# Token tiles 2 and 3 turned on TensorE instead of by DMA, and a new order of loads and queries, in the opening of an attention and MLP kernel

## The chip, the cores and the metric

The kernel runs on one core of one Trainium2 chip. The metric is the device time of the execution in microseconds. Before the change its median is 1055.08 us of 3 runs (1054.37 to 1055.83).

## What is computed

The reference, cut to what matters (S = 2048 tokens, D = 1024, 32 heads of 32, F = 3584, all bf16):

```python
def reference(A_x, A_wqkv, A_wo, B_x, B_w1, B_b1, B_w2, B_b2):
    x = A_x
    xn = _layernorm(x)
    # A: attention on xn
    q, k, v = split_heads(xn @ A_wqkv)
    p = softmax(q @ k.T * 32 ** -0.5)           # 32 heads, 2048 x 2048 each
    s = merge_heads(p @ v) @ A_wo
    # B: MLP on layernorm(xn)
    h = gelu(_layernorm(xn) @ B_w1 + B_b1)
    g = silu(h @ B_w2 + B_b2)
    return x + s * g
```

## The kernel before

The kernel lists its operations with what each reads and writes, lets a small scheduler written in Python put them in an order per engine while it is built, and then emits that order with semaphore waits. The order is static: nothing is chosen on the chip. The durations that the scheduler assumes (for a DMA, for an engine's operation) only serve to choose the order.

In the opening, x is loaded in 16 tiles of 128 tokens. For each tile DVE (VectorE) takes mean and variance, GpSimd the power -0.5, and DVE writes the normalized tile in bf16 (tile 2's sums are taken on ACT, ScalarE). The matmuls need the tile turned (features on the partitions), and for that there are two ways:

```python
def tr_item(t, half=None):              # on TensorE, in a PSUM bank
    ...
        for dc in range(lo, lo + n):
            ins = e.transpose(bankb(b)[:, dc * 128:(dc + 1) * 128],
                              xnb[t % 4][:, dc * 128:(dc + 1) * 128], ident[:])
    ...
    if half == 1 or t in EVD:           # and a copy to the turned tokens xnT
        dve(lambda e: e.tensor_copy(dst, src()), ...)
    else:
        act(lambda e: e.activation(dst, src(), ACT.Copy), ...)
# ...
for t in (lo, lo + 1):                  # the tiles of pair n
    if t < TD:                          # TD = 2 before
        pro_q.append(tr_item(t))
    else:                               # by DMA
        add("SP", lambda e, t=t: e.dma_start_transpose(
                out=xnT[:, :, t * 128:(t + 1) * 128], in_=xnb[t % 4]),
            1290, 0, [("xnb", t % 4)], [("xnT", t, h) for h in range(2)], 0,
            sem=f"tp{t % 4}", nbytes=262144)
pro_q.append(k_pair_item(n, False))     # keys of the pair, first head group
if n == 1:
    pro_q.append(q_pair_item(1))        # queries of the second 256 tokens
if n >= VLAG:                           # VLAG = 2
    pro_q.append(v_item(0, n - VLAG, "pro"))   # values, two pairs behind
```

Heads are worked four at a time (a head group), queries in groups of 256 tokens, keys in pairs of tiles (256 keys). A unit is one query group against one key pair: its scores are 8 matmuls on PE (TensorE, L1167), and its exponentials two activations of 128x1024 on ACT (L1181). The first two query groups go through the key pairs together, so that each new pair gives ACT two units, or four activations; query group 2 starts when pair 7, the last, is through. The kernel has 8 head groups x 8 query groups x 8 pairs = 512 units, so 1024 activations. Products with the values are 8 matmuls (L723), while matmuls of the projections, MLP and output (L728) are put between the scores.

```python
for tq in range(1, 4):                  # queries of the first head group, 512 tokens each
    it = qk_item(0, 0, tq, wq0, 16 * tq - 12)
    if tq == 1 and QE:                  # QE = 0 before
        ...
    plan.queues["proj"].append(it)

def load_w1(p):                         # first weights of the MLP, in two halves of 256 KB
    ...
        dma(f"w1{gi}{i}", ..., [xnop[XW + 2 * p]] if p < 3 else [])   # waits for a normalized tile
def load_w2(q, r):                      # second weights, 448 KB each
    ...
    dma(f"w2{i}", lambda e: e.dma_start(w2r[:, i], src), 580000, [], [("w2", i)])
```

Where PE would find nothing to do early in the kernel, the order may have a matmul of the identity as filler. All DMA is issued from SP (SyncE).

Of the kernel before, what the change touches and what calls it, by code (L numbers as in the profile page):

```python
# [42 lines left out]
NCUT = 2  # L43
HALF = 1
NU = 22
QE = 0
AS = (2,)
FILL = 300
ADJ2 = 0
TD = 2  # L50
XA = 8
XB = 5
XW = 9
ENGS = ("PE", "ACT", "DVE", "POOL", "SP")


# [18 lines left out]
class _Plan:  # L75
# [54 lines left out]
    def run(self, total_units, dense_slack):  # L130
# [28 lines left out]
        def commit(o, t):  # L159
            e = o.eng  # L160
            o.start = t
            if e == "SP":
                if o.prio >= 5:
                    for x in reversed(order["PE"]):
                        if x.fin <= t:
                            o.deps[x] = True
                            break
                tf[e] = t + o.occ
                state["bw"] = max(state["bw"], t) + o.nbytes / 380.0
                o.fin = state["bw"] + {"w1": WLAT, "w2": WLAT, "tp": 2800.0, "x0": 2050.0, "x1": 2000.0, "x2": 2500.0}.get(o.sem[:2], 2300.0)  # L170
            else:
                tf[e] = t + o.occ
                o.fin = t + o.occ + o.lat
            order[e].append(o)
            self.seq.append(o)
            release(o, t)
            wake(tf[e], e)
# [379 lines left out]
def bass_recurrent_scan__mha_block__mixer_channel_mlp__prompt_kernel(  # L557
# [39 lines left out]
    with ExitStack() as st:  # L597
# [112 lines left out]
        def pool(fn, occ, R, W, prio=3):  # L710
            return add("POOL", fn, occ, PL, R, W, prio)

        def dma(sem, fn, nbytes, R, W, prio=3, extra=()):
            return add("SP", fn, 430, 0, R, W, prio, sem=sem, nbytes=nbytes, extra=extra)

        def chunk(item, fn, occ, R, mode="f", W=()):
            o = add("PE", lambda e, fn=fn, item=item: fn(e, item.bank), occ, TL, R, W, item=item, mode=mode)
# [36 lines left out]
        def load_v(pr):  # L754
            src = A_wqkv[:, 2 * D + pr * 256: 2 * D + (pr + 1) * 256].rearrange("(c p) n -> p c n", p=128)
            dma("wv", lambda e: e.dma_start(wv, src), 850000, [], [("wv",)])
# [2 lines left out]
            load_x(t)  # L759
        wk0 = load_qk(0, 1)  # L760
        wq0 = load_qk(0, 0)
        for t in range(XF, 6):
            load_x(t)
        load_v(0)
        for t in range(6, XA):
            load_x(t)
        pool(lambda e: e.iota(iota_i, pattern=[[1, 128]], base=0, channel_multiplier=-1), 300, [], [("iota",)])
        dve(lambda e: e.tensor_single_scalar(ident[:], iota_i, 0, op=ALU.is_equal), 220, [("iota",)], [("ident",)], 0)
        dve(lambda e: e.memset(ones[:], 1.0), 90, [], [("ones",)], 0)
# [35 lines left out]
        def q_pair_item(n):  # L805
            return pair_item(n, (0,))
# [77 lines left out]
        for n in range(NPR):  # L884
            for t in (2 * n, 2 * n + 1):
                if t in AS:

                    junk = yT[:, 4:8, :].rearrange("p c t -> p (c t)")
                    act(lambda e, t=t: e.activation(junk, xst[t], ACT.Copy, scale=-1.0 / 32768, accum_out=lnp[:, t, 2:3]),
                        c_acts(1024) + 93, [XS(t)], [("yT", 2), ("yT", 3), ("st", t, 0)], 1)  # L890
                    act(lambda e, t=t: e.activation(junk, xst[t], ACT.Square, bias=lnp[:, t, 2:3], scale=1.0 / 32,
                                                    accum_out=mv[:, t, 1:2]),
                        c_acts(1024) + 186, [XS(t), ("st", t, 0)], [("yT", 2), ("yT", 3), ("st", t, 1)], 1)
                    dve(lambda e, t=t: e.tensor_scalar_mul(mv[:, t, 0:1], lnp[:, t, 2:3], -32.0), 65,
                        [("st", t, 0), ("st", t, 1)], [("mv", t)], 1)
                else:
                    for c in range(2):
                        dve(lambda e, t=t, c=c: e.bn_stats(stats[:, t, c, :], xst[t][:, c * 512:(c + 1) * 512]),  # L898
                            600, [XS(t)], [("st", t, c)], 1)
                    dve(lambda e, t=t: e.bn_aggr(mv[:, t, :], stats[:, t, :, :].rearrange("p c s -> p (c s)")),  # L900
                        150, [("st", t, 0), ("st", t, 1)], [("mv", t)], 1)
                for k in range(XA, NT):
                    if max(0, k - XB) == t:
                        load_x(k, [("st", t, 0)])
            lo, hi = 2 * n, 2 * n + 2
            if n == 0:
                for t in (0, 1):
                    dve(lambda e, t=t: e.tensor_scalar_add(lnp[:, t:t + 1, 0], mv[:, t:t + 1, 1], EPS), 90, [("mv", t)], [("ve", 0, t)], 0)
                    pool(lambda e, t=t: e.tensor_tensor(lnp[:, t:t + 1, 1], lnp[:, t:t + 1, 0], mhalf[:, t:t + 1], op=ALU.pow),
                         650, [("ve", 0, t), ("mhalf",)], [("rs", 0, t), ("rs", 0)], 0)  # L910
                    dve(lambda e, t=t: e.tensor_scalar(xnb[t], xst[t], mv[:, t, 0:1], lnp[:, t, 1:2],
                                                       op0=ALU.subtract, op1=ALU.mult), 455,
                        [XS(t), ("mv", t), ("rs", 0, t)], [("xnb", t)], 0.5)
                pro_q += [tr_item(0), qk_tile_item(0), tr_item(1, 0), tr_item(1, 1), qk_tile_item(1)]
                if VLAG == 0:
                    pro_q.append(v_item(0, 0, "pro"))
                continue
            dve(lambda e, lo=lo, hi=hi: e.tensor_scalar_add(lnp[:, lo:hi, 0], mv[:, lo:hi, 1], EPS), 90,
                [("mv", lo), ("mv", lo + 1)], [("ve", n)], 1)
            dve(lambda e, lo=lo, hi=hi: e.tensor_scalar_mul(lnp[:, lo:hi, 4], mv[:, lo:hi, 0], -1.0), 65,  # L920
                [("mv", lo), ("mv", lo + 1)], [("nm", n)], 1)
            pool(lambda e, lo=lo, hi=hi: e.tensor_tensor(lnp[:, lo:hi, 1], lnp[:, lo:hi, 0], mhalf[:, lo:hi], op=ALU.pow),
                 700, [("ve", n), ("mhalf",)], [("rs", n)], 0)
            pool(lambda e, lo=lo, hi=hi: e.tensor_tensor(lnp[:, lo:hi, 5], lnp[:, lo:hi, 4], lnp[:, lo:hi, 1], op=ALU.mult),
                 200, [("nm", n), ("rs", n)], [("nb_", n)], 0)
            for t in (lo, lo + 1):
                if t in DN:
                    xnop[t] = dve(lambda e, t=t: e.tensor_scalar(xnb[t % 4], xst[t], mv[:, t, 0:1], lnp[:, t, 1:2],
                                                                 op0=ALU.subtract, op1=ALU.mult), 455,
                                  [XS(t), ("mv", t), ("rs", n)], [("xnb", t % 4)], 0.5)  # L930
                    continue
                xnop[t] = pool(lambda e, t=t: e.tensor_scalar(xnb[t % 4], xst[t], lnp[:, t, 1:2], lnp[:, t, 5:6],
                                                    op0=ALU.mult, op1=ALU.add), 950,
                     [XS(t), ("nb_", n), ("rs", n)], [("xnb", t % 4)], 1)
            for t in (lo, lo + 1):
                if t < TD:
                    pro_q.append(tr_item(t))
                else:

                    add("SP", lambda e, t=t: e.dma_start_transpose(out=xnT[:, :, t * 128:(t + 1) * 128], in_=xnb[t % 4]),  # L940
                        1290, 0, [("xnb", t % 4)], [("xnT", t, h) for h in range(2)], 0, sem=f"tp{t % 4}", nbytes=262144)
            pro_q.append(k_pair_item(n, False))
            if n == 1:
                pro_q.append(q_pair_item(1))
            if n >= VLAG:
                pro_q.append(v_item(0, n - VLAG, "pro"))
        for n in range(NPR - VLAG, NPR):
            pro_q.append(v_item(0, n, "pro"))
        q_at = len(pro_q)

        pool(lambda e: e.tensor_tensor(lnp[:, :, 2], mv[:, :, 1], lnp[:, :, 1], op=ALU.mult), 150,
             [("rs", n) for n in range(NPR)], [("s2",)], 2)
# [22 lines left out]
        def load_w1(p):  # L975
            gi = p % NW1R
            pi = p % NW1
            for i in range(2):
                src = B_w1[i * 512:(i + 1) * 512, pi * 256:(pi + 1) * 256].rearrange("(c p) f -> p c f", p=128)
                dma(f"w1{gi}{i}", lambda e, i=i, src=src: e.dma_start(w1r[gi][:, 4 * i:4 * i + 4], src), 332000, [], [("w1", gi, i)], 3,  # L980
                    [xnop[XW + 2 * p]] if p < 3 else [])

        def load_w2(q, r):
            i = nw2["n"] % NW2R
            nw2["n"] += 1
            src = B_w2[r * 7 * 128:(r + 1) * 7 * 128, q * 256:(q + 1) * 256].rearrange("(f p) n -> p f n", p=128)
            dma(f"w2{i}", lambda e: e.dma_start(w2r[:, i], src), 580000, [], [("w2", i)])
            return i

        def b1_item():  # L990
# [349 lines left out]

        for tq in range(1, 4):
            it = qk_item(0, 0, tq, wq0, 16 * tq - 12)
            if tq == 1 and QE:
                it.kind, it.due = "pro", 1
                pro_q.insert(q_at - QE, it)
                continue
            plan.queues["proj"].append(it)
            it.after = 1000
# [144 lines left out]
```

The softmax here doesn't subtract the row's maximum and nothing guards it: scores larger than these inputs give would overflow.

## Time and profile before

| | before |
|---|---|
| median of 3 runs | 1055.08 us |
| profiled span | 1055.5 us |
| busy: PE / ACT / DVE / GpSimd | 1028.4 / 1013.0 / 960.5 / 14.8 us |
| instructions | 32143 |
| DMA moved | 160.16 MB |

The profile is one execution. Its page gives the busy time of each engine, the span in 40 equal slices (a digit is the busy share of a slice in tenths, PEclk the clock that TensorE was granted), the chain of work that ended last, and groups of instructions by line: count, busy time, mean duration, and after the second bar the idle time before them with what ended it. Durations of pipelined instructions overlap: an activation of 128x1024 shows some 1.02 us alone, but a row of them comes every 0.92 us. A matmul of 256 columns shows 0.27 us, and a row of them comes about every 0.11 us. Names such as `big<-gw` say what is written from what: `big` holds the turned tokens, `gw` and `yT` the normalized tiles before turning, `qk` the weights, queries and keys of the first head group, `w1r` and `w2r` the MLP's weights, `P` the exponentials, `hT` and `w2r` early on also x.

### The profile page before, as it was taken

The page shows a single profiled execution, that of the slowest core. Times are in us where ns is not written, and L with a number is a line of the kernel's source. Part 1 is how long each engine was busy: PE and PEld are TensorE (multiplying, and loading weights), DVE is VectorE, ACT ScalarE, POOL GpSimd, SP SyncE. Part 2 cuts the span into 40 slices and gives each one's busy share as a digit, 9 for nine tenths or more (in the row PEclk, how much of TensorE's full clock was granted, in tenths as well). Part 3 has the DMA queues.
Part 4 walks back from the last instruction along what each step waited for, and adds up shares of the span by engine and source line. Part 5 has one row for each costly group of instructions (what it writes and reads, how often), then busy time and mean ns, then how long its engine had stood idle before and what let it go on. Part 6 is the DMA issues. An engine that isn't in the chain of part 4 may idle for free.

```text
span 1055.5 us, 32143 instructions
## 1 busy us (share of the span) xinstructions
PE 1028.4 (97%) x14326; PEld 637.6 (60%) x14326; DVE 960.5 (91%) x1454; ACT 1013.0 (96%) x1104; POOL 14.8 (1%) x28
## 2 busy tenths in 40 slices
PE   8899999999999999999999999999999999999997
PEld 4445566656676566656676566656665667664442
DVE  7659999999899999999999999999989999979897
ACT  4699999999999999999999999999999999999993
POOL 1200000000000000000000000000000000000000
PEclk9999999999999999999999999999999999999999
DMA  9945256743276356634465456434475587673431
GB/s 234 186 111 148 79 161 191 197 127 96 70 221 173 108 148 185 173 109 113 117 189 161 113 164 183 141 104 116 143 198 161 171 236 221 205 221 95 137 102 60
DMA packets 302371, 160.16 MB, mean 152 GB/s; under 512 B 40218, under 2 KB 293146, under 8 KB 302234
## 3 DMA queue, kind: packets, MB, share of 16 engines
q1 hardware_dynamic: 302234, 158.12, 53.8%
q8 instruction: 112, 1.84, 0.7%
q14 instruction: 25, 0.20, 0.1%
HBM read 142.35 MB, written 12.06 MB: 146 GB/s over the span
## 4 chain that ended last, share of the span: by engine, by line
ACT 85%; PE 11%; DMA 2%; DVE 1%; SPq 0%; issue 0%; DVEq 0%
ACT P L1181 79%; PE ps L728 7%; ACT ut L1042 5%; PE ps L723 2%; PE ps L1167 2%; ACT gw L1078 1%; DMA big<-gw 1%; DMA big<-yT 1%; DMA hT<-in_A_x_dram 0%; DVE w1r L1328 0%; DVE ut L898 0%; SPq L742 0%; PE ps L866 0%; DVE V L1331 0%; DVE V L1328 0%
## 5 line engine op out<-in xcount | busy, mean ns | idle before, releaser
L1181 ACT ACTIVATE P<-ps 128x1024 bf16<-128x1024 f32 x1024 | 964.8, 1241 | 20.3 <-PE ps L1167 20.2
L1211 DVE TENSOR_TENSOR PA<-P 128x2048 bf16<-128x2048 bf16 x245 | 297.7, 1217 | 17.8 <-ACT P L1181 16.5
L728 PE MATMUL ps<-yT,w1r 128*128 128x256 bf16 x1792 | 232.5, 273 | 0.6 <-DVE yT L1010 0.6
L728 PE MATMUL ps<-w2r,hT 128*128 128x256 bf16 x1792 | 225.0, 273 | 1.8 <-DVE xb L1027 0.6
L728 PEld LDWEIGHTS ps<-yT,w1r 128*128 128x128 bf16 x1792 | 162.7, 98 | 56.2 <-issue 30.6
L728 PEld LDWEIGHTS ps<-w2r,hT 128*128 128x128 bf16 x1792 | 163.8, 98 | 50.8 <-issue 29.6
L723 PE MATMUL ps<-P,V 128*32 128x256 bf16 x4096 | 144.7, 274 | 1.2 <-DVE xb L1027 0.7
L728 PE MATMUL ps<-big,qk 128*128 128x512 bf16 (+2 forms) x568 | 133.4, 361 | 6.1 <-DMA big<-gw 3.8
L1216 DVE TENSOR_TENSOR PA<-PA 128x1024 bf16<-128x1024 bf16 x201 | 135.6, 681 | 1.2
L728 PE MATMUL ps<-qk,big 128*128 128x256 bf16 (+1 forms) x736 | 128.0, 308 | 0.9 <-DMA qk<-in_A_wqkv_dram 0.8
L723 PEld LDWEIGHTS ps<-P,V 128*32 128x32 bf16 x4096 | 97.2, 96 | 34.2 <-issue 23.6
L1167 PE MATMUL ps<-qk 32*128 32x256 bf16 x2048 | 108.6, 274 | 6.0 <-ACT P L1181 5.4
L1167 PE MATMUL ps<-QKT 32*128 32x256 bf16 x2048 | 101.7, 273 | 1.4 <-ACT P L1181 1.2
L728 PEld LDWEIGHTS ps<-qk,big 128*128 128x128 bf16 x736 | 65.2, 98 | 44.8 <-issue 19.2
L1027 DVE TENSOR_TENSOR xb<-ps,b1T 128x512 bf16<-128x512 f32 x112 | 76.4, 684 | 8.4 <-PE ps L728 7.1
L728 PEld LDWEIGHTS ps<-big,qk 128*128 128x128 bf16 x568 | 47.8, 98 | 57.4 <-issue 17.3
L1167 PEld LDWEIGHTS ps<-qk 32*128 32x128 bf16 x2048 | 32.2, 92 | 75.6 <-ACT P L1181 69.0
L1167 PEld LDWEIGHTS ps<-QKT 32*128 32x128 bf16 x2048 | 30.3, 92 | 70.9 <-ACT P L1181 67.8
L1042 ACT ACTIVATE ut<-ut 128x1024 f32<-128x1024 f32 x56 | 71.8, 1282 | 0.0
L1045 DVE SCALAR_TENSOR_TENSOR hT<-ut,xb 128x1024 bf16<-128x1024 f32 x56 | 67.9, 1212 | 1.3 <-ACT ut L1042 0.8
L1040 DVE SCALAR_TENSOR_TENSOR ut<-hT,xb 128x1024 f32<-128x1024 bf16 x56 | 67.9, 1215 | 0.0
L1261 DVE STREAM_TRANSPOSE nt<-ps 128x256 f32<-128x256 f32 x64 | 28.6, 446 | 22.8 <-PE ps L723 22.6
(82 smaller groups left out, 539.6 us busy)
## 6 DMA issues: line engine op xcount, KB each, us to landing
w1r<-in_B_w_dram SPq DMA_DIRECT2D x224, 256.0 KB, 3.5
w2r<-in_B_w_dram SPq DMA_DIRECT2D x128, 448.0 KB, 4.4
qk<-in_A_wqkv_dram SPq DMA_DIRECT2D x16, 256.0 KB, 3.2
g_scratch<-gw SPq DMA_DIRECT2D x32, 128.0 KB, 3.1
o_scratch<-ot SPq DMA_DIRECT2D x56, 64.0 KB, 3.1
big<-o_scratch SPq DMA_DIRECT2D x28, 128.0 KB, 3.7
hT<-in_A_x_dram SPq DMA_DIRECT2D x10, 256.0 KB, 5.3
qk<-in_A_wqkv_dram SPq DMA_DIRECT2D x4, 512.0 KB, 3.7
```

What stands on the lines that cost most here:

```text
L723: ins = e.matmul(dst(j), lhsT=lhsT(j), rhs=rhs(j), start=start, stop=stop, tile_position=(0, 32 * j), skip_group_check=True)
L728: return e.matmul(dst, lhsT=lhsT, rhs=rhs, start=start, stop=stop, skip_group_check=True)
L1027: dve(lambda e: e.tensor_tensor(xb_t[i2][:, p % 2].rearrange("p (k t) -> p k t", k=2), bank(it.bank).rearrange("p (k t) -> p k t", k=2), b ...
L1040: dve(lambda e, r=r: e.scalar_tensor_tensor(ut_t[i2][:, r], h[:, r], 1.0 / GA, xb[:, r], op0=ALU.add, op1=ALU.mult), c_f32(r.stop - r.star ...
L1042: act(lambda e: e.activation(ut_t[i2][:], ut_t[i2][:], ACT.Tanh, scale=GC * GA), c_acts(1024), [("ut", i2, 0), ("ut", i2, 1)], [("ut", i2, ...
L1045: dve(lambda e, r=r: e.scalar_tensor_tensor(h[:, r], ut_t[i2][:, r], 1.0, xb[:, r], op0=ALU.add, op1=ALU.mult), c_f32(r.stop - r.start), [ ...
L1078: act(lambda e: e.activation(zh, z, ACT.Tanh, scale=0.5), c_acts(1024), [("z", 0), ("z", 1)], [("zh",)], 1)
L1167: ins = e.matmul(bank(b0[j], kk * 256, (kk + 1) * 256), lhsT=QKT[sl][32 * j:32 * j + 32, 1, kb * 128:(kb + 1) * 128], rhs=QKT[sl][32 * j:3 ...
L1181: x = act(lambda e, h=h: e.activation(P[pi][:, 2 * h:2 * h + 2].rearrange("p j k q -> p (j k q)"), ps[:, pr[h] * 1024:(pr[h] + 1) * 1024], ...
L1211: add2.append(dve(lambda e, p0=p0, a0=a0: e.tensor_tensor(PA_all[:, a0:a0 + 2].rearrange("p u j q -> p (u j) q"), P_all[:, p0:p0 + 2, :, 0 ...
L1216: add4.append(dve(lambda e, a0=a0: e.tensor_tensor(PA[a0], PA[a0], PA[a0 + 1], op=ALU.add), c_b16(1024), [("PA", a0 + 1)], [("PA", a0)], P ...
L1261: a = dve(lambda e: e.transpose(nt_t[i][:], bank(pv.bank, 256, 512)), 368, [], [("nt", i)], 1, pv)
```

## The change

It sets three things anew and adjusts the durations that the scheduler assumes for DMA:

- TD from 2 to 4: tiles 2 and 3 too are turned on TensorE, and copied to `xnT` by ACT. They are the tiles of pair 1.
- The first loads of w2 get a wait for a normalized tile (tile 13), which they had not, and w1's waits are capped at the last tile (their values stay 9, 11 and 13).
- QE from 0 to 5: queries of the second 512 tokens (query groups 2 and 3) become a part of the opening, behind the keys of pair 5 in its list and ahead of the values in rank. Before, they stood in the list of the projections.

WVT places the load of the values' weights; with 6 it stands where it stood. The diff:

```diff
--- before.py
+++ after.py
@@ -43,14 +43,15 @@
 NCUT = 2
 HALF = 1
 NU = 22
-QE = 0
+QE = 5
 AS = (2,)
 FILL = 300
 ADJ2 = 0
-TD = 2
+TD = 4
 XA = 8
 XB = 5
 XW = 9
+WVT = 6
 ENGS = ("PE", "ACT", "DVE", "POOL", "SP")
 
 
@@ -167,7 +168,10 @@
                             break
                 tf[e] = t + o.occ
                 state["bw"] = max(state["bw"], t) + o.nbytes / 380.0
-                o.fin = state["bw"] + {"w1": WLAT, "w2": WLAT, "tp": 2800.0, "x0": 2050.0, "x1": 2000.0, "x2": 2500.0}.get(o.sem[:2], 2300.0)
+                o.fin = state["bw"] + {"w1": WLAT, "w2": WLAT, "tp": 2700.0, "x0": 2050.0, "x1": 2000.0, "x2": 2800.0,
+                                           "wv": 3000.0}.get(o.sem[:2], 2500.0)
+                if o.sem == "x3":
+                    o.fin += 900.0
             else:
                 tf[e] = t + o.occ
                 o.fin = t + o.occ + o.lat
@@ -710,8 +714,11 @@
         def pool(fn, occ, R, W, prio=3):
             return add("POOL", fn, occ, PL, R, W, prio)
 
+        t_dma = [0]
+
         def dma(sem, fn, nbytes, R, W, prio=3, extra=()):
-            return add("SP", fn, 430, 0, R, W, prio, sem=sem, nbytes=nbytes, extra=extra)
+            t_dma[0] += 1
+            return add("SP", fn, 430 if t_dma[0] < 9 else 620, 0, R, W, prio, sem=sem, nbytes=nbytes, extra=extra)
 
         def chunk(item, fn, occ, R, mode="f", W=()):
             o = add("PE", lambda e, fn=fn, item=item: fn(e, item.bank), occ, TL, R, W, item=item, mode=mode)
@@ -759,11 +766,12 @@
             load_x(t)
         wk0 = load_qk(0, 1)
         wq0 = load_qk(0, 0)
-        for t in range(XF, 6):
+        for t in range(XF, XA):
+            if t == WVT:
+                load_v(0)
             load_x(t)
-        load_v(0)
-        for t in range(6, XA):
-            load_x(t)
+        if WVT >= XA:
+            load_v(0)
         pool(lambda e: e.iota(iota_i, pattern=[[1, 128]], base=0, channel_multiplier=-1), 300, [], [("iota",)])
         dve(lambda e: e.tensor_single_scalar(ident[:], iota_i, 0, op=ALU.is_equal), 220, [("iota",)], [("ident",)], 0)
         dve(lambda e: e.memset(ones[:], 1.0), 90, [], [("ones",)], 0)
@@ -938,15 +946,16 @@
                 else:
 
                     add("SP", lambda e, t=t: e.dma_start_transpose(out=xnT[:, :, t * 128:(t + 1) * 128], in_=xnb[t % 4]),
-                        1290, 0, [("xnb", t % 4)], [("xnT", t, h) for h in range(2)], 0, sem=f"tp{t % 4}", nbytes=262144)
+                        1290, 0, [("xnb", t % 4)], [("xnT", t, h) for h in range(2)], 0, sem=f"tp{t % 4}", nbytes=330000)
             pro_q.append(k_pair_item(n, False))
             if n == 1:
                 pro_q.append(q_pair_item(1))
+            if n == QE:
+                q_at = len(pro_q)
             if n >= VLAG:
                 pro_q.append(v_item(0, n - VLAG, "pro"))
         for n in range(NPR - VLAG, NPR):
             pro_q.append(v_item(0, n, "pro"))
-        q_at = len(pro_q)
 
         pool(lambda e: e.tensor_tensor(lnp[:, :, 2], mv[:, :, 1], lnp[:, :, 1], op=ALU.mult), 150,
              [("rs", n) for n in range(NPR)], [("s2",)], 2)
@@ -978,13 +987,13 @@
             for i in range(2):
                 src = B_w1[i * 512:(i + 1) * 512, pi * 256:(pi + 1) * 256].rearrange("(c p) f -> p c f", p=128)
                 dma(f"w1{gi}{i}", lambda e, i=i, src=src: e.dma_start(w1r[gi][:, 4 * i:4 * i + 4], src), 332000, [], [("w1", gi, i)], 3,
-                    [xnop[XW + 2 * p]] if p < 3 else [])
+                    [xnop[min(XW + 2 * p, NT - 1)]] if p < 3 else [])
 
         def load_w2(q, r):
             i = nw2["n"] % NW2R
             nw2["n"] += 1
             src = B_w2[r * 7 * 128:(r + 1) * 7 * 128, q * 256:(q + 1) * 256].rearrange("(f p) n -> p f n", p=128)
-            dma(f"w2{i}", lambda e: e.dma_start(w2r[:, i], src), 580000, [], [("w2", i)])
+            dma(f"w2{i}", lambda e: e.dma_start(w2r[:, i], src), 580000, [], [("w2", i)], 3, [xnop[min(XW + 4, NT - 1)]])
             return i
 
         def b1_item():
@@ -1340,9 +1349,9 @@
 
         for tq in range(1, 4):
             it = qk_item(0, 0, tq, wq0, 16 * tq - 12)
-            if tq == 1 and QE:
-                it.kind, it.due = "pro", 1
-                pro_q.insert(q_at - QE, it)
+            if tq == 1:
+                it.kind, it.due = "pro", 0.5
+                pro_q.insert(q_at, it)
                 continue
             plan.queues["proj"].append(it)
             it.after = 1000
```

## The prediction

> **What bounds the kernel now.** I read the page's busy shares first, then the ACT row of the 40 slices, then what ACT waited for, then ACT in order of time over the first 60 us, and last what PE and the DMA queue were doing at each hole found there.
>
> ```profile
> PE 1028.4 (97%) x14326; PEld 637.6 (60%) x14326; DVE 960.5 (91%) x1454; ACT 1013.0 (96%) x1104; POOL 14.8 (1%) x28
> ACT  4699999999999999999999999999999999999993
> L1181 ACT ACTIVATE P<-ps 128x1024 bf16<-128x1024 f32 x1024 | 964.8, 1241 | 20.3 <-PE ps L1167 20.2
> ```
>
> The first line shows three engines over 90%. The mean alone doesn't say which one sets the end; the other two lines do. ACT (ScalarE) does 1024 exponentials, and in its row only the first two slices (of 26.4 us) and the last are not full. A table of stages confirms it: ACT is busy 100.00 of 100 us from 100 to 200, 200.00 of 200 from 200 to 400, and so on up to 1020. So the end is where the ACT stream ends plus a fixed tail: the last exponentials end at 1039.2 us, and 16.3 us of output projection, additions and stores follow. The stream's length is fixed (86 exponentials in 79.37 us near the end, 0.923 us each). What can move the end is when the stream becomes gapless, and that is decided in the first 60 us. ACT in order of time there (start, length, what, idle before and its releaser):
>
> ```profile
> 22.09 5.61 ACT L1181 ACTIVATE P<-ps 128x1024 bf16<-128x1024 f32 x6 [5.51 <-PE ps L1167]
> 28.31 3.77 ACT L1181 ACTIVATE P<-ps 128x1024 bf16<-128x1024 f32 x4 [0.62 <-PE ps L1167]
> 32.32 3.81 ACT L1181 ACTIVATE P<-ps 128x1024 bf16<-128x1024 f32 x4 [0.24 <-PE ps L1167]
> 38.66 3.77 ACT L1181 ACTIVATE P<-ps 128x1024 bf16<-128x1024 f32 x4 [2.53 <-PE ps L1167]
> 44.35 1.94 ACT L1181 ACTIVATE P<-ps 128x1024 bf16<-128x1024 f32 x2 [1.92 <-PE ps L1167]
> 49.11 1.02 ACT L1181 ACTIVATE P<-ps 128x1024 bf16<-128x1024 f32 x1 [2.83 <-PE ps L1167]
> 54.61 1.02 ACT L1181 ACTIVATE P<-ps 128x1024 bf16<-128x1024 f32 x1 [1.46 <-PE ps L1167]
> 58.30 1.94 ACT L1181 ACTIVATE P<-ps 128x1024 bf16<-128x1024 f32 x2 [0.56 <-PE ps L1167]
> ```
>
> Each group of four is one pair of token tiles becoming keys; the last line starts pair 7, and after it ACT never waits until the tail. The holes from 22.09 on sum to 16.8 us (5.51+0.62+0.24+2.53+1.92+2.83+0.48+0.48+1.46+0.17+0.56; the short ones are in the same answer). That is the most the change can win. Two holes have a DMA transpose behind them:
>
> ```profile
> 13.02 6.74 DMA big<-yT
> 42.39 5.48 DMA big<-gw
> ```
>
> These lines of the chain say that tile 3 took 6.74 us and tile 13 took 5.48 us from issue to landing. The DMA queue in time:
>
> ```profile
> 37.85 1.13 SPq L980 DMA_DIRECT2D w1r<-in_B_w_dram  x2
> 39.02 0.52 SPq L987 DMA_DIRECT2D w2r<-in_B_w_dram  x1
> 40.32 6.93 SPq L940 DMA_TRANSPOSE big<-gw  x3
> 47.29 1.31 SPq L940 DMA_TRANSPOSE big<-yT  x1
> ```
>
> Three transposes took 6.93 us to issue, where two took 2.67 us at 18.82: a 448 KB piece of w2 stands directly ahead of them. While PE waited for tile 13 (2.83 us, to 47.91) its clock fell:
>
> ```profile
> 46.00:48.00 2.00, 0.09 (x1) 0.09 (x2) 0.48 (x2) 0.28 (x1) 0.38 (x1) 1.00 1.23 276
> 48.00:50.00 2.00, 2.00 (x14) 0.81 (x16) 0.00 (x0) 0.89 (x1) 0.00 (x0) 0.59 0.88 168
> 50.00:55.00 5.00, 5.00 (x49) 2.07 (x52) 1.12 (x2) 2.58 (x4) 0.00 (x0) 0.50 0.70 203
> ```
>
> The columns are PE, PEld, DVE, ACT and POOL busy, granted clock, DMA share and GB/s. At half clock PE fed ACT only 2.58 us of work in 5.
>
> **What the Trainium skill says.** *TensorE: Matmul & The Clock Gate*, Part 4, says that a TensorE transpose lands in PSUM and needs a copy out, and measured about 275 ns in a kernel. Here one of 128x128 shows 219 ns, eight overlapped take 0.62 us, and ACT's copy of a tile 1.02 us. The same page ("Why this matters for your kernels") warns of gaps over about 3 us returning the clock to half; the trace agrees, with the clock at 0.50 after a gap of 2.83 us. *DMA: Bandwidth & Descriptors*, "Rules for kernel authors", says that all issuing engines share the same 16 DMA engines; so a weight load and a transpose compete, as the 6.93 us suggest without proving.
>
> **The change, part by part.** In the built instruction order, ACT, DVE, PE and SP differ only in the opening and in a few places of no weight later (one matmul moved past a score, some prefetches swapped). So I work only the opening.
>
> *Tiles 2 and 3 by TensorE.* Added: 16 transposes (2 x 0.62 us PE), two ACT copies (2 x 1.02 us, one ahead of the first exponential and one after it). Removed: two DMA transposes. In the old order PE also stood until 13.77 for the values' weights ahead of the first scores; in the new one these scores go first. DVE, re-ordered, normalizes tiles 0 and 1 about 0.7 and 1.1 us earlier, but tiles 2 and 3 about 1 us later (tile 2 at 12.0 instead of 11.05), as statistics of tile 4 come ahead. From the durations: tile 3 normalized at 13.3; transposed at 13.95; copied between the first two exponentials, to 16.05; values and 3 more matmuls occupy PE to 16.1; keys of pair 1 by 17.0; its DVE copy, behind a values copy (0.6), one statistics half (0.6) and tile 4 (0.45), ends at 18.1; scores at 18.25; exponential at 18.7 instead of **22.09: 3.4 us earlier**. The ACT copies cost nothing, for they lie in a hole.
>
> *What is passed on.* From here DVE sets the rhythm: a tile pair costs it four statistics halves (4 x 0.6), two normalizations (2 x 0.46), a keys copy (0.34), a values copy (0.6) and some 0.4 of small operations, 4.7 us, more than the 3.7 us of its four exponentials. DVE waited little before (1.64 us at 20.89 and 1.07 at 37.35 were its main waits after 16 us), so most of the 3.4 us can't be carried. Going through the new DVE and PE orders with the same durations and about 4 us per DMA transpose (median to landing 3.9), I get the first exponential of pair 2 at 25.7 (28.31 before), pair 3 at 31.0 (32.32), pair 4 at 35.6 (38.66) and pair 5 at 42.3 (44.35); in this last stretch PE is the limit, 11 us of matmuls between the scores of pairs 3 and 5.
>
> *w2 behind the transposes.* Tiles 12 and 13 now stand behind one w1 piece only; a w1 piece ahead of tiles 10 and 11 earlier cost them little (issues of 1.24 and 1.70 us). DVE delivers them near 37.5 (39.76 and 40.2 before), so they land at 42 to 43.5, about when PE is through with pair 5. PE's 2.83 us wait falls below 1.5 us, and the clock probably doesn't drop. From pair 6's keys to pair 7's scores PE then has some 7.0 us of matmuls at full clock, about as long as the 8 exponentials of pairs 5 and 6 (7.4 us). Pair 7 starts on ACT at 42.3+7.4 = 49.7 if nothing is lost, 50.5 with the small gaps of before (0.17, 0.56), 51.2 with a rest of the wait. *Queries of groups 2 and 3* were in the old order already at 32.58 as gap fillers; their eight 512-column matmuls stay there, three of them behind pair 4's keys. That is worth next to nothing alone.
>
> **Sum.** 58.30 - 51.2 = 7.1 us earlier on a stream that afterwards is the same and gapless: 1055.1 - 7.1 = 1048.0 us.
>
> **Rivals.** *A: DVE or PE eats it.* If DVE keeps its old pace in tiles 12 to 15, only the old waits of 3.4 us at tile 3 and the little that DVE had idle come back, and the clock still drops: 2 to 3 us, 1052.5. For it: DVE is busy 4.85 to 5.00 of 5 us between 25 and 35. Against: pair 7 came 15 us after tile 15 was normalized (42.9), so the end of the opening was not DVE's. *B: the wait only moves.* w1's third piece now goes out between tiles 13 and 14, where before it went after 15; if it holds up tiles 14 and 15, PE waits at pair 7 and the clock drops there: 1051 to 1053. Against: 8 exponentials lie in stock by then. *C: PE becomes the bound later.* It is busy 98 to 100% in every stage, so the earlier stream could run into PE. Against: the PE order and ACT's work are the same from pair 7 on, and ACT never waited there, so both merely shift.
>
> **Range and chances.** Without any loss the sum gives 1046 to 1047; with rival A or B 1051 to 1053. I take 1048.0 with 1045.0 to 1052.5. A gain of over 2% (21 us) exceeds the 16.8 us of holes; a loss of 21 us would need a new stall in the steady stage, which the unchanged order doesn't offer: 0.01 each.
>
> **What would show it.** Right: the first pair-1 exponential near 18.7; no wait of PE over 1.5 us between 40 and 50; clock 1.00 from 45 to 55; ACT gapless from about 51; the stages after 60 unchanged and the tail again about 16 us. Wrong: a PE wait for tile 13 or 15 followed by a clock of 0.5 (B), or pairs 4 to 6 at their old times with DVE without idle time (A), or ACT holes after 60 us (C). If the clock drops in one place, I'd be some 3 us too low.

## The result, and the profile after

The changed kernel takes 1049.61 us (median of 4 runs, 1049.19 to 1049.87) against 1055.45 us of the kernel before beside it (1054.37 to 1059.37): a ratio of 0.9938, with a 95% interval of 0.9912 to 0.9963. That is 5.8 us less. The prediction was 1048.0 us, in a range of 1045.0 to 1052.5.

From the page after, the ACT row of the 40 slices and the group of the exponentials:

```profile
ACT  6799999999999999999999999999999999999993
L1190 ACT ACTIVATE P<-ps 128x1024 bf16<-128x1024 f32 x1024 | 964.6, 1241 | 9.5 <-PE ps L1176 9.4
```

The exponentials are as long as before (964.6 us busy). Their waits for scores fell from 20.3 to 9.5 us, and hardly anything later moved: ACT is again busy 200.00 of 200 us in each of the three stages from 200 to 800, its last exponential ends at 1031.4, and the tail to 1047.4 is 16.0 us (16.3 before). ACT after, in order of time (start, length, what, idle before and its releaser):

```profile
18.15 5.61 ACT L1190 ACTIVATE P<-ps 128x1024 bf16<-128x1024 f32 x6 [1.75 <-PE ps L1176]
24.86 3.77 ACT L1190 ACTIVATE P<-ps 128x1024 bf16<-128x1024 f32 x4 [1.11 <-PE ps L1176]
29.90 2.85 ACT L1190 ACTIVATE P<-ps 128x1024 bf16<-128x1024 f32 x3 [1.27 <-PE ps L1176]
34.74 3.77 ACT L1190 ACTIVATE P<-ps 128x1024 bf16<-128x1024 f32 x4 [0.49 <-PE ps L1176]
41.30 1.94 ACT L1190 ACTIVATE P<-ps 128x1024 bf16<-128x1024 f32 x2 [2.79 <-PE ps L1176]
43.98 2.85 ACT L1190 ACTIVATE P<-ps 128x1024 bf16<-128x1024 f32 x3 [0.75 <-PE ps L1176]
50.50 20.43 ACT L1190 ACTIVATE P<-ps 128x1024 bf16<-128x1024 f32 x22 [0.51 <-PE ps L1176]
```

The first line starts pair 1, the next ones pairs 2 to 5, the line at 43.98 the rest of pair 5 and the first of pair 6, and the last one pair 7: gapless from 50.50 instead of 58.30. The DMA queue after:

```profile
35.86 4.38 SPq L948 DMA_TRANSPOSE big<-gw  x2
40.28 1.13 SPq L989 DMA_DIRECT2D w1r<-in_B_w_dram  x2
41.46 1.33 SPq L948 DMA_TRANSPOSE big<-gw  x1
42.83 1.53 SPq L948 DMA_TRANSPOSE big<-yT  x1
44.40 0.74 SPq L996 DMA_DIRECT2D w2r<-in_B_w_dram  x1
```

PE's wait for tile 13 after (start, length, what, idle before and its releaser):

```profile
42.35 1.05 PE L735 MATMUL ps<-big,qk 128*128 128x256 bf16 x8 [1.08 <-DMA big<-gw]
```

And by stage the length, then PE, PEld, DVE, ACT, POOL busy, granted clock, DMA share and GB/s. The first line is the kernel before, the other two are the kernel after:

```profile
45.00:50.00 5.00, 2.17 (x15) 0.90 (x16) 0.48 (x2) 2.17 (x3) 1.38 (x1) 0.84 0.88 187
45.00:50.00 5.00, 5.00 (x71) 2.80 (x68) 1.11 (x2) 4.69 (x6) 0.00 (x0) 1.00 0.94 239
50.00:55.00 5.00, 5.00 (x76) 2.82 (x75) 0.69 (x1) 4.50 (x5) 0.00 (x0) 1.00 1.13 278
```

w2 goes behind the last transpose, PE waits 1.08 us for tile 13 instead of 2.83, and its clock stays at 1.00. From 45 to 50 ACT is busy 4.69 us where it had 2.17.

The spans of the two profiles differ by 8.1 us, the medians by 5.8. The difference is in the kernel before: its profiled execution took 1057.32 us. (A span is some 1.8 us shorter than the time of the same execution, so its span of 1055.5 us looks like the median and isn't.) Beside the experiments the kernel before ran 93 times, with a median of 1055.1 us and times from 1051.2 to 1060.1. Where that spread comes from is a part of the answer. One more number helps there: for every execution the clock that TensorE was granted is recorded as a mean over the span. In the profiled execution before it is 0.995, in the four after 0.998 to 0.999.

### The profile page after: what moved, and what is told of

It is laid out like the page before. It is cut to its first block, busy times and chain, and to the rows that moved or that the text cites. A ratio compares the mean times of both kernels' runs of the same rounds, so it can differ in the third digit from the quotient of the medians.

```text
span 1047.4 us, 32171 instructions
## 1 busy us (share of the span) xinstructions
PE 1024.9 (98%) x14340; PEld 638.1 (61%) x14340; DVE 960.2 (92%) x1454; ACT 1014.6 (97%) x1106; POOL 14.6 (1%) x28
## 4 chain that ended last, share of the span: by engine, by line
ACT 86%; PE 10%; DVE 2%; DMA 1%; SPq 0%; issue 0%; DVEq 0%
ACT P L1190 79%; PE ps L735 6%; ACT ut L1051 5%; PE ps L1176 2%; PE ps L730 2%; ACT gw L1087 1%; DVE ut L906 1%; DMA big<-gw 1%; DMA hT<-in_A_x_dram 1%; DVE gw L936 0%; DVE w1r L1337 0%; DVE V L806 0%; SPq L749 0%; DVE qk L834 0%; SPq L757 0%
## 5 line engine op out<-in xcount | busy, mean ns | idle before, releaser
L1190 ACT ACTIVATE P<-ps 128x1024 bf16<-128x1024 f32 x1024 | 964.6, 1241 | 9.5 <-PE ps L1176 9.4
```

Of the source, the lines that this page charges most:

```text
L1190: x = act(lambda e, h=h: e.activation(P[pi][:, 2 * h:2 * h + 2].rearrange("p j k q -> p (j k q)"), ps[:, pr[h] * 1024:(pr[h] + 1) * 1024], ...
```

## The experiments

Each was timed beside the kernel before on the same chip, if nothing else is said; ratios are against it, with a 95% interval. Three theories stood against each other: the gain comes from tiles 2 and 3, it comes from w2's place behind the transposes, or it comes from the instruction order that the new assumed durations bring.

### Tiles 2 and 3 on TensorE alone

```diff
-TD = 2
+TD = 4
```

> The kernel before with tiles 2 and 3 turned on TensorE, nothing else. The theory (tile 3's DMA transpose was the one long wait early on, and DVE's rhythm carries part of its gain to the end of the opening): first exponential of pair 1 near 18 to 19 us instead of 22.1, ACT gapless from 52 to 54, time 1050.5 to 1052. The rival (the opening is ended by tiles 12 to 15, whatever tile 3 does): pairs 4 to 7 at their old times, 1054 to 1055.5.

Measured: 1054.84 us (1051.32 to 1057.95), ratio 1.0005 (0.999 to 1.002): **no gain** that could be seen. ACT in order of time, and then one stage (columns as above):

```profile
17.67 5.80 ACT L1181 ACTIVATE P<-ps 128x1024 bf16<-128x1024 f32 x6 [0.84 <-PE ps L1167]
40.98 1.94 ACT L1181 ACTIVATE P<-ps 128x1024 bf16<-128x1024 f32 x2 [2.35 <-PE ps L1167]
47.06 1.02 ACT L1181 ACTIVATE P<-ps 128x1024 bf16<-128x1024 f32 x1 [4.14 <-PE ps L1167]
55.81 11.10 ACT L1181 ACTIVATE P<-ps 128x1024 bf16<-128x1024 f32 x12 [0.51 <-PE ps L1167]
```

```profile
45.00:50.00 5.00, 5.00 (x30) 2.09 (x29) 1.50 (x4) 2.05 (x2) 0.00 (x0) 0.53 1.09 253
```

Pair 1 starts at 17.67 and pair 5 at 40.98, as early as in the changed kernel. Then a hole of 4.14 us opens: PE has got to the keys of pair 6 earlier and waits longer for their tiles (3.7 us), and after the longer wait the clock is down to 0.53. Against an execution of the kernel before that kept its clock (shown further below), PE is through with its work ahead of the wait 1.8 us earlier (41.2 against 42.9), while tile 13 lands only 0.6 us earlier (44.78 against 45.41). (On the page before, where all was later from pair 1 on, it landed at 47.87.) And the clock falls more often: all 14 executions have a mean clock of 0.997 or less, while 16 of the 43 of the kernel before beside them have 0.998 or more. The earlier start was real, and it was lost in a longer wait and in the clock.

### w2 behind the transposes alone

```diff
-            dma(f"w2{i}", ..., 580000, [], [("w2", i)])
+            dma(f"w2{i}", ..., 580000, [], [("w2", i)], 3, [xnop[min(XW + 4, NT - 1)]])
```

> The kernel before with w2's first piece issued after the last transposes instead of ahead of tiles 12 to 14; no other instruction moves. The theory of the prediction (that piece holds the transposes up): three issues in under 5 us instead of 6.93, tile 13 landed 4 us after its issue instead of 5.48, PE's wait under 1.5 us, no drop of the clock, 1051.5 to 1053.5. The rival (a transpose issue stalls by itself, with little else under way): issue and landing times as before, 1054.5 to 1055.5.

Measured: 1050.87 us (1050.26 to 1051.49), ratio 0.9959 (0.9945 to 0.9973). ACT in order of time, then the DMA queue in order of time, then a piece of the chain:

```profile
20.68 5.61 ACT L1181 ACTIVATE P<-ps 128x1024 bf16<-128x1024 f32 x6 [5.51 <-PE ps L1167]
51.21 14.93 ACT L1181 ACTIVATE P<-ps 128x1024 bf16<-128x1024 f32 x16 [0.51 <-PE ps L1167]
```

```profile
38.65 4.62 SPq L940 DMA_TRANSPOSE big<-gw  x3
```

```profile
39.93 3.74 DMA big<-gw
```

The hole before pair 1 is as large as before (5.51 us), and still pair 7 starts at 51.21. 1.4 us of the 7.1 us to the page before were there at pair 1 (20.68, not 22.09), ahead of the first instruction that the edit moves. The last two lines show the rest: three transposes issue in 4.62 us instead of 6.93, and tile 13 lands 3.74 us after its issue instead of 5.48. PE's longest wait for a transpose is 1.3 us and the clock is 1.00. One move of one DMA issue gives 3.9 us, two thirds of the change, and the times of its 5 executions lie within 1.3 us, where the 43 of the kernel before beside them spread over 8.

### Both together, and the durations alone

The first kernel has the two edits above and nothing more of the change.

> The kernel before with both: tiles 2 and 3 on TensorE, and w2's first loads behind the transposes; no new durations, no new place for the queries. If these two make the change: pair 1 near 18, no wait of PE over 1.5 us for tiles 12 and 13, clock 1.00 throughout, 1049 to 1050.5, as the changed kernel. If the order that comes from the durations or the queries matters: 1051 to 1053.

Measured: 1049.15 us (1048.2 to 1056.1), ratio 0.9944 (0.9928 to 0.996), the same as the change within the intervals. One of its 15 executions is the 1056.1, with a mean clock of 0.991 where the others have 0.998 or 0.999: the drop of the clock has become rare, and not impossible. The second has only the assumed durations:

```diff
-  {..., "tp": 2800.0, ..., "x2": 2500.0}.get(o.sem[:2], 2300.0)
+  {..., "tp": 2700.0, ..., "x2": 2800.0, "wv": 3000.0}.get(o.sem[:2], 2500.0)   # x3 + 900
-  return add("SP", fn, 430, ...)
+  return add("SP", fn, 430 if t_dma[0] < 9 else 620, ...)                       # tp: 330000
```

> The kernel before with the scheduler's assumed DMA durations of the changed kernel, nothing else. They reorder the start of PE's list: the first scores stand ahead of the matmuls with the values' weights. Theory: the first exponential comes some 0.6 us earlier into a hole that stays (it ends with tile 3's transpose), so 1054.5 to 1055.5. Rival (the order that follows from the durations is itself the gain): 1052 or less.

Measured: 1055.87 us (1051.51 to 1059.86), ratio 1.0013 (1.0 to 1.0025): no gain. So of all that the diff touches, two things make the time. The queries' new place by itself moves no instruction in the kernel before; and as tiles and w2 alone reach the change's time, the intervals leave nothing for it to explain. In the changed kernel w2's wait isn't what holds w2 back either: built without that wait, its DMA issues come in the same order, because with tiles 2 and 3 on TensorE the new durations already make the scheduler put w2 behind.

### Tiles 2 and 3 by DMA again in the changed kernel

```diff
-TD = 4
+TD = 2
```

> The changed kernel with tiles 2 and 3 turned by DMA again, w2 still behind the transposes. If TensorE's part is worth only what the runs so far leave for it (w2's place alone gave 4 of 5.5 us): pair 1 near 20.5, pair 5 near 42.5, pair 7 near 51.2, 1050.3 to 1051.5. If it is worth its 2.5 to 3.4 us once tiles 12 and 13 come in time: 1052 to 1053.

The changed kernel itself, beside it on the same chip:

> The changed kernel, unchanged, on the chip of the three other runs of this group, so that they can be set against it: 1049 to 1050, with a spread of under 1.5 us, as its waits of PE stay near 1 us and its clock doesn't drop.

Measured: the changed kernel 1049.06 us (0.9941, 0.9927 to 0.9956); with tiles 2 and 3 by DMA 1051.4 us (1050.03 to 1053.39; 0.9962, 0.9947 to 0.9977). So with w2 out of the way TensorE's part is worth about 2.3 us by the medians, though the intervals overlap. The profiles give 1.5: pair 7 at 51.31 against 49.86, from a start of pair 1 at 20.74 against 17.88; another execution of the changed kernel has pair 7 at 50.50, so single profiles settle this to some 0.6 us only.

### The kernel before with its clock held, and a second execution of it

To part the wait for tiles 12 and 13 from the drop of the clock that follows it, PE gets work in this wait: 11 matmuls of the identity into the bank that pair 6's keys then overwrite.

```diff
-            for s, v in self.waits[o]:
+            ws = self.waits[o]
+            if o is self.keep:           # first matmul of pair 6's keys
+                ...                      # waits other than those for the transposes
+                self.keep_fn(eng, o.item.bank)   # 11 x identity, 128x512
+                ws = [...]               # the waits for the transposes
+            for s, v in ws:
                 eng.wait_ge(sems[s], v)
```

> The kernel before with 11 matmuls of the identity put on PE where it waits for tiles 12 and 13 (2.4 us of work in a wait of 2.83), so that the wait stays and its consequence for the clock goes. If the drop of the clock to 0.5 cost ACT the holes after 50 us: clock 1.00 from 45 to 55, ACT gapless 2 to 3 us earlier, 1052 to 1053.5. If ACT would have had these holes at full clock too, or if the drop is rare: 1054.5 to 1055.5.

And a second profiled execution of the kernel before:

> The kernel before, unchanged, profiled once more. If its spread from execution to execution comes from the clock: an execution near 1051 to 1053 shows no drop after 48 us and a shorter wait for tiles 12 and 13, one at 1055 or more shows a drop to 0.5.

Measured: with the clock held 1052.52 us (1051.67 to 1053.23; 0.9978, 0.9967 to 0.9988); the second execution of the kernel before took 1051.96 us. Of the kernel with its clock held first ACT in order of time and then one stage, and after them the same two of the second execution:

```profile
47.57 2.85 ACT L1192 ACTIVATE P<-ps 128x1024 bf16<-128x1024 f32 x3 [2.63 <-PE ps L1178]
54.08 12.94 ACT L1192 ACTIVATE P<-ps 128x1024 bf16<-128x1024 f32 x14 [0.51 <-PE ps L1178]
```

```profile
45.00:50.00 5.00, 4.51 (x46) 2.13 (x47) 1.60 (x4) 2.43 (x3) 0.02 (x1) 1.00 0.97 216
```

```profile
46.43 2.85 ACT L1181 ACTIVATE P<-ps 128x1024 bf16<-128x1024 f32 x3 [2.30 <-PE ps L1167]
52.95 23.18 ACT L1181 ACTIVATE P<-ps 128x1024 bf16<-128x1024 f32 x25 [0.51 <-PE ps L1167]
```

```profile
45.00:50.00 5.00, 4.54 (x64) 2.35 (x64) 1.12 (x2) 3.27 (x4) 0.00 (x0) 1.00 0.93 220
```

With the clock held ACT's hole is still there (2.63 us), so the wait stays; what goes is what came after it, 2.2 us by the medians, and most of the spread (1.6 us instead of 8). The kernel with w2 moved takes 1050.87 us beside the same executions of the kernel before, so by these medians w2's 3.9 us are some 2.2 of clock and 1.7 of the shorter wait itself.

The second execution is the unchanged kernel with good luck: PE waits 2.5 us for tile 13 and the clock holds, and pair 7 starts at 52.95, not at 58.30. Not all of these 5.35 us are the clock's. Pair 5 already starts at 42.20 instead of 44.35, and pair 1 at 20.08 instead of 22.09: on the page tile 3's transpose goes out 0.8 us later (13.02, here 12.25) and takes 1.2 us longer to land (6.74, here 5.50). What comes between pairs 5 and 7, where the clock fell, is 3.2 us.

So the kernel before stands at an edge: its wait of 2.5 to 2.8 us brings the clock down in some executions and not in others. The mean clocks say how often. Of its 93 executions 20 have 0.998 or 0.999, as the second execution, and took 1051.2 to 1053.7 us, with a median of 1052.3; the other 73 have 0.996 or less, as the execution on the page before, and took 1052.9 to 1060.1, with a median of 1055.4. The page on which the prediction was built shows the usual case, in an execution in which pair 1 also came late.

### What the changed kernel leaves

Two runs vary what is loaded ahead of the transposes in the changed kernel; only DMA issues move in both. First all weights of the MLP behind tile 15:

```diff
-XW = 9
+XW = 15
```

> The changed kernel with all loads of w1 and w2 after tile 15 is normalized; only DMA issues move. If any load ahead of a transpose holds it up: tiles 12 and 13 issue in 2.7 us instead of 4.4 and land by 41.3 instead of 42.3; PE's rest of a wait (1.1 us) goes; 1048.5 to 1049.3. If transposes stall by themselves: the two issue in over 4 us as before, 1049.3 to 1050.5. If the MLP's first matmuls now wait for w1: ACT holes after 60 us and 1051 or more.

Measured: 1048.44 us (1048.03 to 1048.67), ratio 0.9932 (0.991 to 0.9953). ACT in order of time:

```profile
41.58 7.62 ACT L1190 ACTIVATE P<-ps 128x1024 bf16<-128x1024 f32 x8 [2.79 <-PE ps L1176]
49.70 25.93 ACT L1190 ACTIVATE P<-ps 128x1024 bf16<-128x1024 f32 x28 [0.51 <-PE ps L1176]
```

Pairs 5 and 6 are one row of 8 exponentials: the wait for tile 13 is gone, pair 7 starts at 49.70, and no hole from late weights follows. The slowest of the transposes issued between 34 and 47 us lands in 4.3 us instead of 5.6, and in 6.6 in the kernel before. They don't become instant with nothing ahead of them (2.8 us at least), and the issues of tiles 12 and 13 still take 3.34 us, more than the 2.7 expected. Of the two transposes issued from 26.48 us on, with a tile of x ahead and no weights of the MLP, one took 5.2 us to land. By their times (ratios 0.9932 and 0.9938) this kernel and the changed one can't be told apart.

Then w2's first piece ahead of the last transposes again, with half a w1 piece behind tile 15 in exchange:

```diff
-  dma(f"w2{i}", ..., 3, [xnop[min(XW + 4, NT - 1)]])
+  dma(f"w2{i}", ..., 3 if nw2["n"] > 1 else -1,
+      [xnop[min(XW + 4, NT - 1) if nw2["n"] > 1 else 11]])
```

> The changed kernel with w2's first piece ahead of the transposes of tiles 12 and 13 again (one half of a w1 piece goes behind the last transpose in its place); only DMA issues move. 704 KB of weights then stand between tiles 11 and 12 instead of 512 in the changed kernel and 960 in the kernel before. If landing follows the bytes ahead: tile 13 some 1 us later than in the changed kernel, PE waits 1.5 to 2.5 us, 1050.3 to 1052, and more spread. If w2 holds them up by its kind and not by its bytes: the wait of 3.7 us of the run with TensorE alone, clock 0.5, 1053 to 1056.

Measured: 1050.05 us (1049.18 to 1057.32), ratio 0.9957 (0.9941 to 0.9973). In the profiled execution tile 13 landed at 42.29 us, as in the changed kernel (42.30), and neither forecast was met. But the forecast had the order wrong: the DMA queue shows w2's piece going out at 32.54 us, between the transposes of tiles 10 and 11, so that directly ahead of tiles 12 and 13 stood only 256 KB of weights, less than the 512 KB of the changed kernel. So the run shows that w2 may go out one transpose earlier with half a w1 piece less behind it; it doesn't test w2 directly ahead of tiles 12 and 13, and whether bytes, place or kind of a load matter stays open. Two of its 12 executions took 1055.9 and 1057.3 us, with mean clocks of 0.991 and 0.993 where the others have 0.998 or 0.999. The changed kernel showed this in none of 10, which is too few to tell the two apart.

### Two attempts to go further

Keys of a pair ahead of the products with the values, to close the hole of 2.79 us before pair 5:

```diff
-                    cands.append((o.ready, 2, o, None))
+                    cands.append((o.ready, 0.5 if it.kind == "pro" and it.due == 0 else 2, o, None))
                     ...                  # and the same where an item takes a new bank
```

> The changed kernel with the keys of a pair going ahead of products with the values on PE in the opening; this changes the scheduler's picks and so also some of the order after the opening. The hole of 2.79 us before pair 5 should close to under 1 us, as PE then doesn't work off 5 us of products first; pair 6 still needs tile 13 (42.3), so pair 7 comes at most 1 us earlier: 1048.3 to 1049.5. If the products put off come back as holes after 50 us, or the later order is worse: 1050 to 1053.

Measured: 1051.97 us (1050.02 to 1055.29), ratio 0.997 (0.9961 to 0.998), slower than the change. ACT in order of time, and then what it waited for after 60 us (total, times, longest):

```profile
39.69 2.85 ACT L1190 ACTIVATE P<-ps 128x1024 bf16<-128x1024 f32 x3 [1.15 <-PE ps L1176]
48.65 9.34 ACT L1190 ACTIVATE P<-ps 128x1024 bf16<-128x1024 f32 x10 [0.40 <-PE ps L1176]
65.58 10.19 ACT L1190 ACTIVATE P<-ps 128x1024 bf16<-128x1024 f32 x11 [1.79 <-PE ps L1176]
```

```profile
ACT P L1190 <- PE ps L730: 1.9, 1, 1.9
```

The hole before pair 5 shrank from 2.79 to 1.15 us, and pair 7 came at 48.65, 1.85 us earlier than in the change. Two holes later took it back and more: 1.8 us at 65 us and 1.9 us at 91 us. The order after the opening had changed too, and there ACT waits for PE; around the second hole, from 85 to 90 us, PE's clock is 0.77.

Tiles 4 and 5 on TensorE too, on top of all weights last:

```diff
-TD = 4
+TD = 6
-XW = 9
+XW = 15
```

> The changed kernel with all weights behind tile 15 and also tiles 4 and 5 turned on TensorE and copied by ACT. The two copies (0.92 us of ACT each) fit into ACT's holes of 1.1 and 1.3 us before pairs 2 and 3, but DVE's rhythm sets the pairs from there, and PE's products pair 5: pair 7 within 0.5 us of 49.7, time 1048 to 1049. If turning without the DMA's 4 us carries further: 1047.5 or less. If the copies push exponentials back: 1049.5 or more.

Measured: **1048.1 us** (1047.5 to 1048.56), ratio 0.9928 (0.9914 to 0.9941), the lowest median of all, with the changed kernel at 1049.06 on the same chip; the two intervals overlap. ACT in order of time:

```profile
48.31 27.76 ACT L1190 ACTIVATE P<-ps 128x1024 bf16<-128x1024 f32 x30 [0.51 <-PE ps L1176]
```

Pair 7 starts at 48.31, 1.4 us before the run with all weights last alone. Some 0.6 us of this is an earlier start of the profiled execution (first exponential at 13.07 against 13.63), which leaves 0.8, more than the 0.5 expected. The ratios of the two runs (0.9928 and 0.9932) can't be told apart, so a gain from tiles 4 and 5 isn't shown.

## Why the prediction was right, and where it was not

**The bound.** Right: ACT's stream after the opening is the same, gapless, and followed by the same tail; rival C fell. Rival B fell too: w1's third piece did go out between tiles 13 and 14, and the hole before pair 7 is 0.51 us, with the clock at 1.00.

**Pair 1 and what is passed on.** Right within 1.1 us: pair 1 at 18.15 (18.7 predicted), pair 2 at 24.86 (25.7), pair 3 at 29.90 (31.0), pair 4 at 34.74 (35.6), pair 5 at 41.30 (42.3), pair 7 at 50.50 (51.2). The ACT copies did lie in a hole. All six came earlier than predicted; the prediction's times rest on the durations of an execution in which pair 1 came late.

**The wait for tile 13 and the clock.** Right: 1.08 us of wait (under 1.5 predicted), clock 1.00. The runs show what the prediction said was not proved: w2 ahead of the transposes held them up (tile 13 lands 3.74 us after its issue without it, 5.48 with it); by what mechanism stays open. That tile 13 landed where it was expected (42.30; 42 to 43.5 predicted) is partly luck: DVE had the two tiles ready at 36.3 us, 1.2 us earlier than worked out, and the transpose of tile 13 took 4.84 us where about 4 were assumed, after an issue of tile 12 that took 1.6 us.

**The sum.** The step that was mis-sized is its last one: 58.30 - 51.2 was taken from a page whose execution had come late to pair 1, had lost its clock and took 1057.32 us, and was subtracted from a median of 1055.1. Subtracted from the page's own time it gives 1057.32 - 7.1 = 1050.2 us, 0.6 us from what was measured. In the second execution pair 7 starts at 52.95, only 2.45 us after the changed kernel's; on the page it is 7.8 us after. The medians, 5.8 us apart, mix both. The page's time stood beside the runs' times, and I didn't set them against each other.

**Which part does it.** The working put the two parts in a row: 3.4 us won at tile 3, most of it used up by DVE, and the rest from w2. The runs show that the first is worth nothing that can be seen without the second (1.0005 alone) and 1.5 to 2.3 us with it, while the second alone is worth 3.9. An earlier start only reached the end of the opening once the wait at its end had moved. Rival A's outcome (a gain mostly eaten, and the clock still dropping) came true for the tiles alone, with another cause: pair 5 had come early (40.98), so DVE did not keep its old pace; the wait for tiles 12 and 13 and the clock after it ate the gain. That w1 pieces ahead cost little held only for the tiles read then: with them behind too, the wait for tile 13 goes, though a gain in time isn't shown.

**Queries.** Right: nothing moves by them alone.

## What to carry to other kernels

An earlier start is worth only what the last wait of that stage lets through: find the wait that ends last, and move what stands ahead of it in its queue, before speeding up what comes first. Loads that are needed much later belong behind the short transfers that something waits for. And before holes are taken from one profile, set the time of that execution beside the other runs: if it lies apart, its holes are not the typical ones.

## What the runs showed of the hardware

A wait of about 2.5 us on TensorE stood at the edge of a clock drop: with 2.5 us the clock stayed at 1.00 in one execution, with 2.83 us it went to 0.50 in another of the same kernel, with 3.7 us it went to 0.53 in the kernel with tiles 2 and 3 alone. The Trainium skill, *TensorE: Matmul & The Clock Gate*, Part 1, describes a window of some 3.4 us that runs freely and doesn't start with the kernel, which would fit an outcome that changes between executions. It asks for a whole idle window, though, and here 2.83 us were enough; the runs don't show the window itself. Eleven matmuls of no use in the wait were worth 2.2 us.

A DMA transpose of 256 KB took 2.7 us at best from issue to landing, up to 5.2 us in the kernel with no weights of the MLP ahead, and up to 7.3 us in the kernel with tiles 2 and 3 alone. In the kernel before, while tile 13's transpose was under way from 44 to 46 us, the DMA moved only 35 GB/s. Why it crawls there stays open.
